# Turning the value matmuls of an attention kernel around (V stationary in four column groups, P streamed) and giving its scores 64 rows

## The chip, the cores and the metric

The kernel runs on one NeuronCore of a Trainium2 chip. The metric is the device time in microseconds, as the median of several executions. All times quoted here are of runs in the normal ("fast") state. Before the change the median was 1947.76 us (two runs, 1946.03 to 1949.48).

Abbreviations: PE is the TensorE (matmuls), PEld its weight loads, DVE the VectorE, ACT the ScalarE, POOL the GpSimd. PSUM is the memory that matmuls write; the kernel uses it as eight banks of 128 x 512 fp32.

## The reference, cut to what matters

```python
def _A_ref(x, wq, wk, wv, wo):           # S = 2048, D = 512, H = 32 heads, Dh = 16
    q = heads(x @ wq); k = x @ wk; v = x @ wv      # one k and one v for all 32 heads
    scores = einsum("bhqd,bkd->bhqk", q, k) * Dh ** -0.5
    p = softmax(scores)
    o = einsum("bhqk,bkd->bhqd", p, v)
    return merge(o) @ wo
# _B_ref: linear attention with H = 32 (cheap); _layernorm in front of each
x = x + A(ln(x));  x = x + B(ln(x));  x = x + A(ln(x));  x = x + B(ln(x))
```

Block A has 2048 x 2048 x 32 exponentials, twice. With 128 keys on the partitions and 512 queries in the free dimension that is 4096 tiles of 128 x 512: each is one score matmul, one exponential, and the value matmuls that consume it.

## The kernel before

A list scheduler in Python simulates the engines at build time with assumed durations, and so fixes the order of instructions on every engine. The order is static on the chip: if an engine is later than the scheduler assumed, the others wait (in `a_moreD` below the PE waits 65 us for the DVE to free score banks).

An exponential has two paths. ACT takes three score tiles at a time (`fill`). The DVE takes pairs of tiles with a polynomial in six passes (`dstep`, `dpass`); whoever is free in the scheduler's simulation takes the next tile.

```python
def smm(self, e, p, b):                       # one score tile: K of 32 rows
    u, kt, j = self.pos[p]
    qb, g, par = self.units[u]
    return e.matmul(bank(b), lhsT=Kr[32 * j:32 * j + 32, par, kt * P:(kt + 1) * P],
                    rhs=QT[32 * j:32 * j + 32, qb % 2, g, :], start=True, stop=True)
...
    def f(e):                                 # in fill: three scores, side by side in the array
        for i, p in enumerate(got):
            k = self.smm(e, p, 3 * s + i)
        return k
    o = add(PE, 0.06 + 0.08 * m, f, reads=self.keys(got), deps=prev, uses=[h], prio=0.0, name="sA")
    ...
    oe = add(AC, tac(m * 512), lambda e: e.activation(PTA[:, hp.idx, 0:m * 512], bank(3 * s, m * 512), ACTF.Exp, scale=SCALE), ...)
...
    def f(e):                                 # in add_pv: P is stationary, V (17 columns) moves
        first = opened[0]
        for qs in range(4):
            i = e.matmul(bank(7, 17, (qs * 4 + j) * 17), lhsT=src(qs), rhs=Vaug[:, kt, 0:17],
                         start=(first and qs == 0), stop=(qs == 3), skip_group_check=True)
        return i
...
    # in norm, after 64 tiles: reciprocal of column 17, product into Osb, from bank 7
```

A head has 16 rows of K. `Kr` holds K with zeros in the rows of the other head of a 32-row strip, so `par` chooses the head.

The softmax here doesn't subtract the row's maximum and nothing guards it: scores larger than these inputs give would overflow.

## Time and profile before

| | before |
|---|---|
| median | 1947.76 us |
| profiled span | 1935.7 us |
| mean granted TensorE clock | 0.575 |
| PE / DVE / ACT busy | 92% / 88% / 88% |
| exponentials on ACT; tiles on the DVE | 1179; 560 |
| idle time of ACT just before exponentials | 117.7 us |

Three views of the page of the kernel before follow. The first lines are busy time and share of each engine, and the granted clock in 40 slices of the span, in tenths of full speed.

```profile
span 1935.7 us, 49030 instructions
...
PE 1778.2 (92%) x22208; PEld 820.9 (42%) x22208; DVE 1712.9 (88%) x3063; ACT 1702.0 (88%) x1330; POOL 45.1 (2%) x77
...
PEclk8555556555665555555975555655565555556559
```

The chain that ended last, by engine:

```profile
PE 57%; DVE 29%; ACT 11%; issue 1%; DMA 0%; POOL 0%; SPq 0%
```

The groups of instructions (line, engine, operation, tiles, shapes, count | busy us, mean ns | idle us of the engine just before, and what ended it):

```profile
L689 ACT ACTIVATE PTA<-ps_all 128x1536 bf16<-128x1536 f32 x1179 | 1625.1, 1464 | 117.7 <-PE ps_all L572 108.8
L572 PE MATMUL ps_all<-QT,Kr 32*128 32x512 bf16 x4096 | 914.0, 582 | 80.0 <-ACT PTA L689 38.8
...
L608 PE MATMUL ps_all<-Vaug,PTA 128*128 128x17 bf16 x14144 | 584.0, 176 | 4.6 <-ACT PTA L689 2.5
L735 DVE TENSOR_SCALAR xT<-ps_all 128x512 int32<-128x512 f32 x560 | 385.1, 688 | 116.1 <-PE ps_all L572 105.1
...
L815 ACT ACTIVATE e_buf<-ps_all 128x512 f32<-128x512 f32 x64 | 37.8, 597 | 39.8 <-PE ps_all L475 38.7
```

Both users of the scores, ACT (L689) and the DVE (L735), idle over 100 us each for score matmuls, and the PE is first in the chain. Yet the TensorE clock is at half speed nearly all the time (digits 5 and 6, mean 0.575). So a slow PE delays two engines that would otherwise be nearly full.

The timeline of the PE at half clock shows what each piece takes (start us, us, engine, line, operation, count):

```profile
150.05 0.61 PE L572 MATMUL ps_all<-QT,Kr 32*128 32x512 bf16 x3
150.59 0.49 PE L608 MATMUL ps_all<-Vaug,PTA 128*128 128x17 bf16 x12
151.01 0.60 PE L572 MATMUL ps_all<-QT,Kr 32*128 32x512 bf16 x1
```

Three 32-row scores take 0.61 us and one takes 0.60: the three run side by side. Subtracting starts, a triple keeps the PE 0.54 us and its twelve value matmuls 0.42 us.

### The profile page before, as it was taken

To read this page: it belongs to the slowest core of one execution; us is meant where nothing else is said; L and a number is where in the kernel's file an instruction comes from. 1 tells how busy PE (TensorE), PEld (TensorE's weight loads), DVE (VectorE), ACT (ScalarE), POOL (GpSimd) and SP (SyncE) were. 2 spreads that over 40 slices of the span, in tenths; PEclk is the share of its full clock that TensorE was granted. 3 is DMA by queue.
4 is the path that set the end of the run, shared out by engine and by line. 5 is a ranking of instruction groups with operands and counts; after the bars stand their busy time and mean duration, and the time that the engine had idled before them with its cause. 6 is when DMAs were issued, how large, how long until landed. Compare 5 with 4: busy or idle time off the path is not lost.

```text
span 1935.7 us, 49030 instructions
## 1 busy us (share of the span) xinstructions
PE 1778.2 (92%) x22208; PEld 820.9 (42%) x22208; DVE 1712.9 (88%) x3063; ACT 1702.0 (88%) x1330; POOL 45.1 (2%) x77
## 2 busy tenths in 40 slices
PE   7999999999999999998889999999999999997977
PEld 4444444444444444443444444444444444443434
DVE  7899989999889988887879999899898989985977
ACT  6999999999989999997589999999998999986973
POOL 2000000000000000000100000000000000000000
PEclk8555556555665555555975555655565555556559
DMA  3000000000000000000000000000000000000001
GB/s 110 2 1 2 2 1 2 2 2 2 1 2 2 2 1 2 2 2 2 1 2 2 2 2 2 2 2 2 1 2 1 2 1 2 2 2 1 2 1 44
DMA packets 7808, 10.50 MB, mean 5 GB/s; under 512 B 1456, under 2 KB 7088, under 8 KB 7600
## 3 DMA queue, kind: packets, MB, share of 16 engines
q1 hardware_dynamic: 7600, 7.37, 1.2%
q8 instruction: 173, 2.83, 0.6%
q14 instruction: 35, 0.29, 0.0%
HBM read 5.28 MB, written 2.10 MB: 4 GB/s over the span
## 4 chain that ended last, share of the span: by engine, by line
PE 57%; DVE 29%; ACT 11%; issue 1%; DMA 0%; POOL 0%; SPq 0%
PE ps_all L572 27%; PE ps_all L608 16%; PE ps_all L475 11%; ACT PTA L689 10%; DVE xT L735 8%; DVE PTD L756 6%; DVE xu L751 3%; DVE xs L755 2%; DVE xs L752 2%; DVE xu L754 1%; DVE xs L753 1%; PE ps_all L920 1%; DVE stats L444 1%; PE ps_all L458 1%; DVE x_sb L931 1%
## 5 line engine op out<-in xcount | busy, mean ns | idle before, releaser
L689 ACT ACTIVATE PTA<-ps_all 128x1536 bf16<-128x1536 f32 x1179 | 1625.1, 1464 | 117.7 <-PE ps_all L572 108.8
L572 PE MATMUL ps_all<-QT,Kr 32*128 32x512 bf16 x4096 | 914.0, 582 | 80.0 <-ACT PTA L689 38.8
L608 PEld LDWEIGHTS ps_all<-Vaug,PTA 128*128 128x128 bf16 x14144 | 470.3, 104 | 566.0 <-issue 552.6
L608 PE MATMUL ps_all<-Vaug,PTA 128*128 128x17 bf16 x14144 | 584.0, 176 | 4.6 <-ACT PTA L689 2.5
L735 DVE TENSOR_SCALAR xT<-ps_all 128x512 int32<-128x512 f32 x560 | 385.1, 688 | 116.1 <-PE ps_all L572 105.1
L756 DVE SCALAR_TENSOR_TENSOR PTD<-xT,xs 128x1024 uint16<-128x1024 int32 x280 | 340.5, 1216 | 1.1
L572 PEld LDWEIGHTS ps_all<-QT,Kr 32*128 32x128 bf16 x4096 | 160.0, 98 | 311.6 <-ACT PTA L689 152.6
L751 DVE TENSOR_SCALAR xu<-xT 128x1024 f16<-128x1024 uint16 x280 | 192.3, 687 | 3.1
L755 DVE TENSOR_TENSOR xs<-xs,xu 128x1024 f16<-128x1024 f16 x280 | 191.0, 682 | 1.4
L752 DVE TENSOR_TENSOR xs<-xu 128x1024 f16<-128x1024 f16 x280 | 190.4, 680 | 0.5
L608 PE MATMUL ps_all<-Vaug,PTD 128*128 128x17 bf16 x2240 | 111.6, 176 | 16.6 <-DVE Osb L625 8.0
L753 DVE TENSOR_SCALAR xs<-xs 128x1024 f16<-128x1024 f16 x280 | 116.4, 416 | 1.0
L754 DVE TENSOR_SCALAR xu<-xu 128x1024 f16<-128x1024 f16 x280 | 117.0, 418 | 0.0
L608 PEld LDWEIGHTS ps_all<-Vaug,PTD 128*128 128x128 bf16 x2240 | 86.1, 104 | 66.8 <-DVE Osb L625 26.9
L475 PE MATMUL ps_all<-wqkv_sb,xnT 128*128 128x512 bf16 x256 | 106.3, 559 | 2.6 <-ACT xnT L464 1.4
L448 POOL TENSOR_TENSOR rstd<-veps,mhalf 128x1 f32<-128x1 f32 x64 | 40.9, 643 | 1842.2 <-DVE veps L446 1623.6
L815 ACT ACTIVATE e_buf<-ps_all 128x512 f32<-128x512 f32 x64 | 37.8, 597 | 39.8 <-PE ps_all L475 38.7
L475 PE MATMUL ps_all<-xnT,wq_sb 128*128 128x512 bf16 x128 | 55.8, 566 | 4.4 <-DVE xT L735 2.1
L475 PE MATMUL ps_all<-xnT,wqkv_sb 128*128 128x512 bf16 x128 | 52.4, 545 | 6.5 <-DVE pqT L818 5.6
L475 PE MATMUL ps_all<-wo_sb,OT 128*128 128x512 bf16 x128 | 51.9, 543 | 2.9 <-ACT OT L799 1.4
L444 DVE BATCH_NORM_STATS2 stats<-x_sb 128x6 f32<-128x512 bf16 x64 | 43.2, 683 | 3.5 <-DMA x_sb<-in_A_x_dram 3.3
L458 PE MATMUL ps_all<-ident,xn_buf 128*128 128x128 bf16 x256 | 31.2, 267 | 15.3 <-DVE xn_buf L451 13.6
(64 smaller groups left out, 625.9 us busy)
## 6 DMA issues: line engine op xcount, KB each, us to landing
out_dram<-x_sb SPq DMA_DIRECT2D x16, 128.0 KB, 1.7
x_sb<-in_A_x_dram SPq DMA_DIRECT2D x3, 512.0 KB, 7.3
wqkv_sb<-in_B_wqkv_dram SPq DMA_DIRECT2D x1, 1536.0 KB, 11.3
x_sb<-in_A_x_dram SPq DMA_DIRECT2D x2, 256.0 KB, 3.5
wq_sb<-in_A_wq_dram SPq DMA_DIRECT2D x1, 512.0 KB, 5.5
wo_sb<-in_A_wo_dram SPq DMA_DIRECT2D x1, 512.0 KB, 8.5
wo_sb<-in_B_wo_dram SPq DMA_DIRECT2D x1, 512.0 KB, 10.9
wk_sb<-in_A_wk_dram SPq DMA_DIRECT2D x1, 16.0 KB, 2.7
```

The source lines that it names most:

```text
L444: add(DV, tdv(512), lambda e: e.bn_stats(stats[:, t, 0:6], x_sb[:, t, :]), reads=[("x", t)], writes=[("st", t)], prio=prio, name="bn")
L475: i = e.matmul(bank(h.idx, n), lhsT=l, rhs=r, start=(c + k == 0), stop=(c + k == len(mms) - 1))
L572: return e.matmul(bank(b), lhsT=Kr[32 * j:32 * j + 32, par, kt * P:(kt + 1) * P], rhs=QT[32 * j:32 * j + 32, qb % 2, g, :], start=True, st ...
L608: i = e.matmul(bank(7, 17, (qs * 4 + j) * 17), lhsT=src(qs), rhs=Vaug[:, kt, 0:17], start=(first and qs == 0), stop=(qs == 3), skip_group_ ...
L689: oe = add(AC, tac(m * 512), lambda e: e.activation(PTA[:, hp.idx, 0:m * 512], bank(3 * s, m * 512), ACTF.Exp, scale=SCALE), deps=[o] + pr ...
L735: o = add(DV, tdv(512), lambda e: e.tensor_scalar(out=xT[:, hx.idx, i * 512:(i + 1) * 512], in0=bank(6), scalar1=SCALE * LOG2E * 65536.0, ...
L751: o = add(DV, tdv(1024, 0.52), lambda e: e.tensor_scalar(out=u_, in0=lo, scalar1=1.0 / 65536, scalar2=-0.5, op0=ALU.mult, op1=ALU.add), de ...
L752: o1 = add(DV, tdv(1024, 0.52), lambda e: e.tensor_tensor(out=s_, in0=u_, in1=u_, op=ALU.mult), deps=[o] + c["prev"], name="xsq", **kw)
L753: o2 = add(DV, tdv(1024, 0.26), lambda e: e.tensor_scalar(out=s_, in0=s_, scalar1=XK, scalar2=-XW, op0=ALU.mult, op1=ALU.add), deps=[o1], ...
L754: o3 = add(DV, tdv(1024, 0.26), lambda e: e.tensor_scalar(out=u_, in0=u_, scalar1=1.0, scalar2=XL, op0=ALU.mult, op1=ALU.add), deps=[o1], ...
L755: o4 = add(DV, tdv(1024, 0.52), lambda e: e.tensor_tensor(out=s_, in0=s_, in1=u_, op=ALU.mult), deps=[o2, o3], name="xc", **kw)
L756: o5 = add(DV, tdv(1024), lambda e: e.scalar_tensor_tensor(out=PTD[:, hp.idx, :].bitcast(U16), in0=xT[:, k, :], scalar=2.0 ** -9, in1=s_, ...
```

## The change

The value matmuls swap operands. V (16 columns, a column of ones and zeros up to 32) becomes the stationary operand in one of four groups of 32 columns of the array, and P streams 512 columns past it. That turns four matmuls per tile into one and is meant to let tiles of different column groups overlap (in the changed kernel three of them take 0.40 us). The result is O transposed, so after 64 tiles the bank is copied to SBUF in fp32, transposed by the PE in fp32, and only then normalised. The scores get 64 rows: K has 64-row strips with zeros in the rows of the other three heads, so only two score matmuls fit side by side instead of three or four. Some buffers shrink to make room.

```diff
-            return e.matmul(bank(b), lhsT=Kr[32 * j:32 * j + 32, par, kt * P:(kt + 1) * P],
-                            rhs=QT[32 * j:32 * j + 32, qb % 2, g, :], start=True, stop=True)
+            i, m = (j % NRG, par * (4 // NRG) + j // NRG)          # RG = 64, NRG = 2
+            r = slice(i * RG, (i + 1) * RG)
+            return e.matmul(bank(b), lhsT=Kr[r, m, kt * P:(kt + 1) * P], rhs=QT[r, qb % 2, g, :], start=True, stop=True)
...
-                for qs in range(4):
-                    i = e.matmul(bank(7, 17, (qs * 4 + j) * 17), lhsT=src(qs), rhs=Vaug[:, kt, 0:17],
-                                 start=(first and qs == 0), stop=(qs == 3), skip_group_check=True)
-                return i
-            o = add(PE, 0.15, f, ...)
+                c = (j % NRG) * (4 // NRG) + j // NRG
+                return e.matmul(ps[32 * c:32 * c + 32, 7 * 512:8 * 512], lhsT=Vaug[:, kt, :], rhs=src, start=opened[0], stop=opened[1],
+                                skip_group_check=True)
+            o = add(PE, 0.1, f, ...)
...  # norm: reciprocal and product came straight from bank 7; now first
+            oe = add((DV, AC), {DV: tdv(512), AC: tac(512)}, ev, deps=[last], acq=[he], uses=[h7], rel=[h7], prio=0.0, name="evA")
+            def tr(e):
+                for qs in range(4):
+                    i = e.transpose(bank(ht.idx, P, qs * P), Eo[:, he.idx, qs * P:(qs + 1) * P], identf[:])
+                return i
...
-            o = add(PE, 0.06 + 0.08 * m, f, ..., name="sA")
+            o = add(PE, 0.05 + 0.14 * m, f, ..., name="sA")
...  # also: four masked copies of K instead of two, smaller buffers, small rules for the
...  # spare PSUM bank and for odd tiles on the DVE, a switch for dummy matmuls (DUMMY = 0.0: off)
```

## The prediction

> **What bounds it now.** In the main attention stretch (100 to 890 us, table by stretches) PE is busy 94%, ACT 93%, DVE 92%, and the granted TensorE clock is 0.54. The groups show 1179 exponentials on ACT, 1625 us busy (1.378 us apiece), with 118 us idle before them, 109 of it waiting for the score matmuls; the DVE's score evictions wait another 105 us for scores. So ACT and DVE carry the exponentials and a slow-clocked PE delays both. The chain of waits gives PE 57%.
>
> [...] The trace agrees: only 0.5 and 1.0 occur, in multiples of 3.41 us. Counting matmuls per window, and weighting a 512-column matmul by the share of array rows that it uses (a score 0.25, a 17-column value matmul 0.033), windows under 5 full matmuls are practically never followed by a full clock (3 of 407), those over 6 usually are. Attention windows hold 3 to 4: hence the half clock.
>
> **What changes.**
> - Value matmuls: 16384 (twelve take 0.42 us at half clock) become 4096 of 512 columns, in four column groups. [...] the trace shows it for rows (three 32-row scores 0.61 us, one 0.60). So three should take one stream: 0.43 us at half clock, 0.22 at full.
> - Scores: only two fit side by side now, so a triple goes from one stream to two: 0.54 to about 0.97 us at half clock, 0.55 at full.
> - [...] I expect the full clock most of the time: mean 0.85 (0.7 to 0.98).
> - PE work per exponential, with projections (estimate): about 2.1 us at half clock, against 1.5 us observed per exponential today; about 1.25 us at full clock. The change stands or falls with the clock.
> - Instruction order: ACT gets 1202 exponentials (+23, +31 us) and 19 more key evictions (+9); DVE loses 63 score tiles (5.48 us per pair, -172 us) and gains 62 fp32 evacuations (0.69 us, +43) and 13 key evictions (+6). ACT's busy time goes to about 1740 us, DVE's to about 1590.
> - 256 fp32 transposes (estimate: [...] off the critical path at full clock).
>
> **Sum.** ACT 1740 + about 116 us of idle outside the exponentials (ends of layers, unchanged) + remaining waits before exponentials, falling from 118 to about 40, gives a span near 1896 us; the timed runs lie about 10 us above the profiled span. Even with no wait at all it would be 1856, so the gain cannot much exceed 4%.
>
> Predicted 1905 us, range 1866 to 1990; faster by over 2%: 0.46, within 2%: 0.33, slower: 0.21.
>
> **What shows it right or wrong.** Mean clock above 0.8 in the attention stretches; score triples near 0.55 us start to value matmul; value triples overlapping fully; idle before exponentials under 60 us, with PE busy about 80%; ACT share 91 to 93%; PE leaving first place in the chain of waits.
>
> **What would make it wrong.** Column groups counting little as activity, so that the clock keeps falling back: [...] at clock 0.6 the time passes 2100. Column groups not overlapping. The accumulator bank now waits for the fp32 copy and the transposes take the spare bank from the DVE path, stalling value matmuls between units. Or the waits before exponentials are not the PE's speed but its fixed order, and stay: then about 1950.

The clock of 0.85 stands as my estimate. The sum at the end: 1740 + 116 + 40 = 1896 us, and about 10 us more for the timed runs. The stream times can be read from the trace of before: four scores in two streams take 1.03 us where three side by side take 0.61, so a stream adds 0.42 us at half clock; at full clock it is 0.60 against 0.39, so 0.21. The estimates of the PE's work per exponential add the projections to the pieces above them. A recount of the windows of that trace has 1 of 400 under 5 followed by a full clock and 69 of 90 over 6; the half-clock windows of the attention stretches hold 4.0 on average.

## The result, and the profile after

The changed kernel takes 1849.78 us (two runs, 1845.92 and 1853.63): 0.9497 of the time before, with a 95% interval of 0.9405 to 0.9589. A later measurement of the same kernel with five runs gave 0.9528 (0.9505 to 0.9551). The direction was right; the time lies 16 us under the stated range, 55 us under the point.

The same lines of the page, for the changed kernel:

```profile
span 1844.2 us, 24784 instructions
...
PE 1608.2 (87%) x10093; PEld 463.8 (25%) x10176; DVE 1617.8 (88%) x2890; ACT 1714.6 (93%) x1373; POOL 47.7 (3%) x80
...
PEclk9999999999999999989999999999999999999999
```

The chain that ended last, by engine:

```profile
DVE 44%; ACT 31%; PE 22%; issue 2%; DMA 0%; POOL 0%; SPq 0%
```

The groups:

```profile
L722 ACT ACTIVATE PTA<-ps_all 128x1536 bf16<-128x1536 f32 x1202 | 1641.8, 1511 | 41.0 <-PE ps_all L590 37.8
L590 PE MATMUL ps_all<-QT,Kr 64*128 64x512 bf16 x4096 | 850.6, 387 | 126.7 <-ACT PTA L722 64.6
L625 PE MATMUL ps_all<-PTA,Vaug 128*32 128x512 bf16 x3599 | 524.9, 392 | 7.0 <-DVE Eo L637 4.5
L776 DVE TENSOR_SCALAR xT<-ps_all 128x512 int32<-128x512 f32 x497 | 341.7, 687 | 83.7 <-PE ps_all L590 82.2
...
L871 ACT ACTIVATE e_buf<-ps_all 128x512 f32<-128x512 f32 x64 | 43.3, 680 | 14.8 <-PE ps_all L490 10.6
...
L646 PE MATMUL ps_all<-identf,Eo 128*128 128x128 f32 x256 | 46.6, 310 | 7.0 <-DVE Eo L637 5.0
```

The clock is now full in almost every slice (mean 0.983 against 0.575). ACT does 23 exponentials more than before and still the time falls, because its idle time before them fell from 117.7 to 41.0 us. The PE left first place in the chain.

The timeline of the PE:

```profile
601.86 0.40 PE L625 MATMUL ps_all<-PTA,Vaug 128*32 128x512 bf16 x3
602.19 0.60 PE L590 MATMUL ps_all<-QT,Kr 64*128 64x512 bf16 x3
602.72 0.40 PE L625 MATMUL ps_all<-PTA,Vaug 128*32 128x512 bf16 x3
```

A triple of 64-row scores keeps the PE 0.53 us, as long as the triple of 32-row scores did at half clock, though it is two streams now. Three value matmuls finish in 0.40 us from first start to last end, about what one score takes alone at full clock (0.39 us in the run a_rg32 below): the column groups overlap. From its first start to that of the next score, a value triple keeps the PE 0.33 us (601.86 to 602.19).

**Where the time came from.** Cutting the span at the first and last exponential of each layer, the two attention stretches went from 889.7 + 917.2 = 1806.9 us to 851.3 + 862.5 = 1713.8 us, 93 us less. The rest of the span (start, between the layers, end) went from 128.8 to 130.4 us. So all of the gain lies inside the attention stretches. There ACT's busy time rose by 11 us and its idle time fell from 146.5 to 42.3 us.

### The profile page after: what moved, and what is told of

Its sections match the earlier page's. It is cut to its first block, busy times and chain, and to the rows that moved or that the text cites. A ratio compares the mean times of both kernels' runs of the same rounds, so it can differ in the third digit from the quotient of the medians.

```text
span 1844.2 us, 24784 instructions
## 1 busy us (share of the span) xinstructions
PE 1608.2 (87%) x10093; PEld 463.8 (25%) x10176; DVE 1617.8 (88%) x2890; ACT 1714.6 (93%) x1373; POOL 47.7 (3%) x80
## 4 chain that ended last, share of the span: by engine, by line
DVE 44%; ACT 31%; PE 22%; issue 2%; DMA 0%; POOL 0%; SPq 0%
ACT PTA L722 29%; DVE xT L776 10%; PE ps_all L590 9%; DVE PTD L798 8%; PE ps_all L625 6%; DVE xs L794 5%; DVE xs L797 5%; DVE xu L793 5%; PE ps_all L490 4%; DVE xu L796 3%; DVE xs L795 2%; PE ps_all L976 1%; PE ps_all L646 1%; DVE Eo L637 1%; ACT e_buf L871 1%
## 5 line engine op out<-in xcount | busy, mean ns | idle before, releaser
L590 PE MATMUL ps_all<-QT,Kr 64*128 64x512 bf16 x4096 | 850.6, 387 | 126.7 <-ACT PTA L722 64.6
L625 PE MATMUL ps_all<-PTA,Vaug 128*32 128x512 bf16 x3599 | 524.9, 392 | 7.0 <-DVE Eo L637 4.5
L590 PEld LDWEIGHTS ps_all<-QT,Kr 64*128 64x128 bf16 x4096 | 176.5, 94 | 574.2 <-ACT PTA L722 251.0
L798 DVE SCALAR_TENSOR_TENSOR PTD<-xT,xs 128x1024 uint16<-128x1024 int32 (+1 forms) x249 | 302.7, 1216 | 1.8
L625 PEld LDWEIGHTS ps_all<-PTA,Vaug 128*32 128x32 bf16 x3599 | 126.0, 93 | 483.2 <-issue 463.9
L793 DVE TENSOR_SCALAR xu<-xT 128x1024 f16<-128x1024 uint16 (+1 forms) x249 | 171.7, 689 | 4.2
L797 DVE TENSOR_TENSOR xs<-xs,xu 128x1024 f16<-128x1024 f16 (+1 forms) x249 | 170.7, 685 | 2.9
L794 DVE TENSOR_TENSOR xs<-xu 128x1024 f16<-128x1024 f16 (+1 forms) x249 | 170.4, 684 | 3.1
L625 PE MATMUL ps_all<-PTD,Vaug 128*32 128x512 bf16 x497 | 136.6, 396 | 31.9 <-DVE PTD L798 18.4
L796 DVE TENSOR_SCALAR xu<-xu 128x1024 f16<-128x1024 f16 (+1 forms) x249 | 104.4, 419 | 0.0
L871 ACT ACTIVATE e_buf<-ps_all 128x512 f32<-128x512 f32 x64 | 43.3, 680 | 14.8 <-PE ps_all L490 10.6
L646 PE MATMUL ps_all<-identf,Eo 128*128 128x128 f32 x256 | 46.6, 310 | 7.0 <-DVE Eo L637 5.0
```

The source lines that it names most:

```text
L590: return e.matmul(bank(b), lhsT=Kr[r, m, kt * P:(kt + 1) * P], rhs=QT[r, qb % 2, g, :], start=True, stop=True)
L625: return e.matmul(ps[32 * c:32 * c + 32, 7 * 512:8 * 512], lhsT=Vaug[:, kt, :], rhs=src, start=opened[0], stop=opened[1], skip_group_check ...
L646: i = e.transpose(bank(ht.idx, P, qs * P), Eo[:, he.idx, qs * P:(qs + 1) * P], identf[:])
L793: o = add(DV, tdv(w, 0.52), lambda e: e.tensor_scalar(out=u_, in0=lo, scalar1=1.0 / 65536, scalar2=-0.5, op0=ALU.mult, op1=ALU.add), deps= ...
L794: o1 = add(DV, tdv(w, 0.52), lambda e: e.tensor_tensor(out=s_, in0=u_, in1=u_, op=ALU.mult), deps=[o] + c["prev"], name="xsq", **kw)
L796: o3 = add(DV, tdv(w, 0.26), lambda e: e.tensor_scalar(out=u_, in0=u_, scalar1=1.0, scalar2=XL, op0=ALU.mult, op1=ALU.add), deps=[o1], nam ...
```

## The experiments

Twelve runs were made, in three jobs: eleven other kernels, and the changed kernel once more (`a_ctl`). The kernel before was timed in each job and had a median of 1939 to 1940 us there. The quoted expectations were put on record before each run. Most set two explanations against each other: the "clock theory" (the gain comes from the full TensorE clock, and the clock follows from how much of the array is at work) and a "rival".

### Each half of the change alone: a_rg32 and b_rg64

`a_rg32` is the changed kernel with 32-row scores again.

```diff
-    RG = 64
+    RG = 32
```

> The changed kernel with its scores back at 32 rows (three scores side by side again, one stream per triple instead of two); value matmuls and instruction order stay (1201 exponentials, 498 DVE score tiles against 1202 and 497). Clock theory (the gain came from the full clock, which the doubled row use of the scores holds): [...] the mean clock falls to 0.5 to 0.65 and the time rises to 1900 to 2050 us, although the PE has fewer streams to do. Rival (fewer and better shaped value matmuls made the gain, whatever the clock): the PE has less work than in the changed kernel, so 1835 to 1860 us.

Measured: 1957.01 us, 1.009 of before (1.0054 to 1.0127), clock 0.766, correct. The turned-around value matmuls alone bring nothing. The clock fell less than expected, but the time is where the clock theory put it, and the rival is off by 100 us. The order of instructions did not stay quite the same: with two masked copies of K instead of four, ACT has 11 instructions fewer and the DVE 21. But a_rg32 has the split of tiles and the scheduler rules of the changed kernel, so these alone do not make its gain. The page shows a clock that comes and goes, and ACT's wait for scores back:

```profile
PEclk8756589867887668958987666998569785787759
```

```profile
L722 ACT ACTIVATE PTA<-ps_all 128x1536 bf16<-128x1536 f32 x1201 | 1656.9, 1489 | 126.7 <-PE ps_all L590 118.6
```

`b_rg64` is the kernel before with 64-row scores alone: `smm`, the masked copies of K and the dependency keys as in the changed kernel. To make room, the buffers PTA, e_buf, xn_buf and Osb2/OT2 are one smaller each.

```diff
+    RG = 64
+    NRG, NM = P // RG, RG // DH
...
+            i, m = (j % NRG, par * (4 // NRG) + j // NRG)
+            r = slice(i * RG, (i + 1) * RG)
+            return e.matmul(bank(b), lhsT=Kr[r, m, kt * P:(kt + 1) * P], rhs=QT[r, qb % 2, g, :], start=True, stop=True)
```

> The kernel before with 64-row scores alone (four masked keys instead of two, value matmuls as before; some buffers one smaller to make room: PTA 5, e_buf 2, xn_buf 2, Osb2/OT2 2; 1182 exponentials, 558 DVE tiles). Clock theory: [...] the clock is unsteady between 0.6 and 0.95 and the time 1850 to 1990 us. Rival (value matmuls made the gain): 64-row scores only add a stream per triple, so slower than before, over 1990 us.

Measured: 2105.66 us, 1.0847 of before (1.0805 to 1.0889), clock 0.686. The output is wrong (relative error 0.21): I had left the order of the heads in the output as it was, while the 64-row strips permute the heads. The work is the same, so only the time is used. It is slower than I gave it credit for: here the prediction of the clock theory (1850 to 1990 us) was wrong and the rival's "over 1990" right. At half clock an exponential took 1.872 us, against 1.533 in before (table below), and the clock stayed at half for two thirds of the attention time (665 exponentials at 1.872 us, 462 at 1.360):

```profile
PEclk8655567565777668755797555679778775767659
```

So of the two halves one costs 1% and the other 8%, and both together gain 5%. The next runs test whether the clock is what joins them.

### Adding useless work: a_rg32_dum, b_dum160

`a_rg32_dum` adds to a_rg32 a matmul with zeros behind every value matmul (the diff leaves out two matmuls at the start, which clear the bank's columns and repeat the first value matmul).

```diff
                 e.matmul(ps[32 * c:32 * c + 32, 7 * 512:8 * 512], lhsT=Vaug[:, kt, :], rhs=src, ...)
+                return e.matmul(bank(7, 160, 272), lhsT=ident[:], rhs=zer[:, 0:160], start=False, stop=True, ...)
```

> The same with one useless 128-row matmul of 160 columns of zeros behind each value matmul (4096 more PE instructions[...]). Clock theory: the clock comes back to over 0.9 and the time to 1840 to 1875 us. If zeros do not count as activity, the clock stays under 0.65 and the time goes above the run without them, 1950 to 2150 us. Rival (PE work decides): slower than the 32-row run without it by 50 us or more.

Measured: 2869.98 us, 1.4793 of before, clock 0.997. This experiment was badly made. The clock was indeed full, but the filler stands between the value matmuls and takes away their overlap, as its timeline shows:

```profile
500.82 0.39 PE L628 MATMUL ps_all<-PTD,Vaug 128*32 128x512 bf16 x1
501.14 0.24 PE L635 MATMUL ps_all<-zer,ident 128*128 128x160 bf16 x1
501.31 0.39 PE L628 MATMUL ps_all<-PTA,Vaug 128*32 128x512 bf16 x1
```

A value matmul now occupies the PE for 0.32 us until the filler starts, and the filler for 0.17 us, so three pairs take 1.47 us. In the kernel before, a further 512-column stream adds 0.21 us at full clock (four scores of which the fourth has no free rows take 0.60 us where three take 0.39, below). Here 0.32 us pass; the trace does not show what the other 0.11 us go to.

```profile
494.28 0.39 PE L572 MATMUL ps_all<-QT,Kr 32*128 32x512 bf16 x3
495.68 0.60 PE L572 MATMUL ps_all<-QT,Kr 32*128 32x512 bf16 x4 [0.61 <-DVE x_sb L809]
```

The run shows that a full clock alone did not help a PE with too much to do: an exponential took 2.27 us at full clock, against 1.366 in a_rg32. It also bears on the question of the zeros: the clock was 0.997 with the filler of zeros and 0.766 without it (a_rg32). So the zeros did not keep the clock at half; that they are what raised it was not shown, since the PE's order of work changed with them.

`b_dum160` adds a filler with real data to the kernel before, where the value matmuls use the whole array anyway. The order of instructions is that of before on every engine.

```diff
-                return i
+                return e.matmul(bank(7, 160, 272), lhsT=ident[:], rhs=wq_sb[:, 0, 0:160], start=False, stop=True, ...)
```

> The kernel before, same order on every engine, with one useless 128-row matmul of 160 columns (weights as data, written to unused columns of the accumulator bank) behind each of the 4096 groups of value matmuls. Clock theory: [...] clock over 0.9, and the kernel gets faster by adding work: 1830 to 1880 us. Rival (the turned-around value matmuls made the gain): the PE was 92% busy, so added work costs time: 1970 to 2150 us.

Measured: 2090.41 us, 1.0764 of before (1.0718 to 1.0809), clock 0.73, correct.

```profile
PEclk9755556977879668876977555978558886895559
```

The clock rose (0.73 against 0.575) but did not stay, and the filler cost PE time: at half clock a group of four value matmuls with its filler kept the PE 0.24 us (0.17 at full), where without it twelve take 0.42, so four 0.14. As a test of the clock alone on the kernel before it failed; the rival's number came out.

### The same work twice: a_rg32_tw, with b_tw as its control

A filler that costs the PE about what the 64-row scores cost is to compute each 32-row triple twice into the same banks: two streams (0.61 us at full clock in this run, as against 0.60 for a 64-row triple in the changed kernel), and as many rows of the array in use, with no useful result in the second.

```diff
-                for i, p in enumerate(got):
-                    k = self.smm(e, p, 3 * s + i)
+                for _ in range(2):
+                    for i, p in enumerate(got):
+                        k = self.smm(e, p, 3 * s + i)
```

> The changed kernel with 32-row scores as in the run a_rg32 (1957 us, clock 0.77), but each ACT score triple is computed twice into the same banks: two streams per triple as in the changed kernel, and the same activity, by pure repetition (about 3600 useless score matmuls). Clock theory: the activity of the changed kernel is back, so the clock is over 0.93 and the time 1840 to 1880 us, faster than a_rg32 by doing the same work twice. Rival (PE work decides, or the 64-row tiles themselves matter): the second pass costs the PE 0.22 to 0.43 us per triple, so 2000 us or more.

Measured: 1874.08 us, 0.9646 of before (0.9599 to 0.9693), clock 0.963, correct. The kernel became 83 us faster than a_rg32 by doing 3598 score matmuls a second time. The rival expected 2000 us or more. Its page, against that of a_rg32 above:

```profile
PEclk9999999999999999998989998999889999899989
```

```profile
L723 ACT ACTIVATE PTA<-ps_all 128x1536 bf16<-128x1536 f32 x1201 | 1645.2, 1502 | 62.0 <-PE ps_all L590 56.9
L590 PE MATMUL ps_all<-QT,Kr 32*128 32x512 bf16 x7694 | 880.0, 389 | 114.2 <-ACT PTA L723 56.6
```

The order of the ACT's and the DVE's instructions is that of a_rg32 from first to last, and the results are right; what differs is the repetition, the clock, and ACT's wait, which halves from 126.7 to 62.0 us. (The two ran in different jobs; their ratios to before, 0.9646 and 1.009, say the same.) It stays 24 us slower than the changed kernel, at a clock of 0.963 against 0.98; why was not tested.

`b_tw` does the same to the kernel before, with its own buffers and right outputs.

> The kernel before, same order on every engine, ACT score triples computed twice: what 64 rows would do to streams and activity, with right outputs and the buffers of before. Control for b_rg64 (2106 us, clock 0.69, smaller buffers, heads of the output permuted). If buffers had no part in it: 2060 to 2140 us, clock 0.6 to 0.75. If the smaller buffers were the cause of its loss: under 1990 us.

Measured: 2181.49 us, 1.1259 of before (1.1211 to 1.1308), clock 0.617, correct. It is slower than the range I gave, but it answers its question: with buffers of full size the second stream costs even more, so the loss of b_rg64 needs no smaller buffers to explain it. With the old value matmuls, more work in the scores did not lift the clock for good (0.617 here, 0.686 in b_rg64, 0.575 in before):

```profile
PEclk8555565556566667755985555755567675555559
```

### The clock within a run

One kernel has both clocks in one execution, with the same order of instructions. Inside the attention stretches (30 us after the first exponential of a layer to 20 us before its last), the trace's records of the clock and of the exponentials give this time per exponential of ACT:

```
               at half clock: us per exponential (count)     at full clock
before         1.533 (1023)                                  1.412 (96)
b_rg64         1.872 (665)                                   1.360 (462)
b_tw           1.862 (865)                                   1.358 (259)
b_dum160       1.912 (550)                                   1.401 (573)
a_rg32         1.688 (505)                                   1.366 (638)
a_rg32_tw      2.35  (48)                                    1.395 (1091)
changed        2.57  (18)                                    1.393 (1124)
```

At the full clock these seven run at nearly the same pace, 1.36 to 1.41 us, though their matmuls differ in shape. At the half clock they differ a lot, from 1.533 to 2.57 us. The half-clock figures of the changed kernel and of a_rg32_tw must not be read as a cost of the clock alone: they rest on 18 and 48 exponentials, and cause and effect run both ways, since the clock also falls where the PE has stalled (in the changed kernel the PE was busy 61% of the window before each of the eight falls in these stretches, 89% of the other full-clock windows). Nor is a full clock enough by itself: at full clock a_rg32_dum takes 2.27 us per exponential, and a_moreD below 1.48. So the change does not make the PE's work cheaper; it makes the PE's clock nearly full (0.983), and at that clock the PE kept up with ACT whether its work was a little more or less (1.366 us per exponential in a_rg32, 1.393 in the changed kernel).

### What the clock went with

The records of the clock hold 0.5 and 1.0 alone, in pieces of 3.41 us or multiples (traces of before and after). How busy the PE is does not set the two apart: in the attention stretches it is busy 94% of the half-clock windows of before, and 89% of the full-clock windows of the changed kernel. In the trace of before the clock went with the work in a window. I counted the matmuls that start in each, in units of 512 columns, weighted by the share of the array's rows that they use, as in the prediction. Of the windows under 5, 1 of 400 was followed by a full clock; from 5 to 6 it was 9 of 72, over 6 it was 69 of 90.

The runs that differ in their matmuls have these mean clocks:

| | old value matmuls | turned around |
|---|---|---|
| 32-row scores | 0.575 (before) | 0.766 (a_rg32) |
| 64-row scores | 0.686 (b_rg64) | 0.983 (changed) |
| 32-row scores, ACT's triples twice | 0.617 (b_tw) | 0.963 (a_rg32_tw) |

So either half of the change raised the clock, but it was nearly full only where the value matmuls were turned around and the scores had 64 rows or were done twice. How much a matmul of each shape counts, and in particular how the 32 columns of a value matmul do, was not shown. That the clock follows the share of the array at work, and not, say, power, is my inference.

### What bounds the kernel now: a_fewD and a_moreD

`a_fewD` tells the scheduler that DVE operations take 1.3 times as long. The chip's DVE is the same; only the split and the order change.

```diff
-        return 0.065 + n * c * 1e-3
+        return 1.3 * (0.065 + n * c * 1e-3)
```

> The changed kernel with the scheduler told that DVE operations take 1.3 times as long, so that its order gives the DVE 396 score tiles instead of 497, and ACT about 1233 exponentials instead of 1202. Theory (at the full clock ACT alone bounds the attention stretch, at 1.33 to 1.37 us per exponential): 31.5 times that, so 40 to 45 us more, 1880 to 1900 us. Rival (PE or DVE still bound it): within 15 us of the changed kernel, or faster since the DVE has 276 us less to do.

Measured: 1888.96 us, 0.9748 of before (0.9723 to 0.9772), clock 0.966, correct. Its span is 45 us longer than that of the changed kernel, for 33 exponentials more (the profile counts 1235), though the DVE's busy time fell by 234 us to 1383.5 us. Of these 45 us, 31 lie in the attention stretches and 14 outside, where the altered durations change the order too. That the total fell into the range is thus partly luck: in the attention stretches 33 exponentials cost 0.94 us each, less than the 1.33 to 1.37 of the theory, because ACT's idle time there fell too, from 42.3 to 35.9 us. The rival is refuted all the same: with 234 us less for the DVE to do the kernel became slower, and the chain that ended last is now ACT's:

```profile
ACT 83%; PE 14%; DVE 2%; issue 1%; DMA 0%; SPq 0%; POOL 0%
```

In the changed kernel the chain names the DVE first (44%), yet ACT is busy in 97.5% of the attention stretches (1671.5 of 1713.8 us), so ACT bounds them.

`a_moreD` uses a factor of 0.9 instead: 536 tiles on the DVE.

> The changed kernel with the scheduler told that DVE operations take 0.9 of its estimate: 536 score tiles on the DVE instead of 497 and 1189 exponentials on ACT instead of 1202. Theory (ACT bounds at 1.33 to 1.37 us per exponential): 13 fewer, so 15 to 18 us faster, if the DVE keeps up; its busy time goes from 1618 to about 1725 us. Rival (DVE is nearly full too, 90% busy in the attention stretch): the gain is lost to waits, 0 to 10 us slower.

Measured: 1970.99 us, 1.0169 of before (1.0128 to 1.0209), clock 0.957, correct. That is 120 us slower than the unaltered changed kernel, far beyond either theory. Its chain and its groups show where:

```profile
DVE 63%; PE 27%; ACT 6%; issue 3%; DMA 0%; POOL 0%; SPq 0%
```

```profile
L722 ACT ACTIVATE PTA<-ps_all 128x1536 bf16<-128x1536 f32 (+1 forms) x1189 | 1644.0, 1458 | 145.4 <-PE ps_all L590 137.2
L590 PE MATMUL ps_all<-QT,Kr 64*128 64x512 bf16 x4096 | 884.4, 395 | 140.2 <-DVE xT L776 65.0
...
L625 PE MATMUL ps_all<-PTD,Vaug 128*32 128x512 bf16 x536 | 145.5, 407 | 73.6 <-DVE PTD L798 46.9
```

ACT is idle 145 us before exponentials, 137 of them for scores, and the PE in turn waits for the DVE: 65 us for a score bank and 47 us for the DVE's probabilities (32.8 and 18.4 us in the changed kernel). The clock is nearly full. The PE takes its instructions in the fixed order, so where that order assumes a DVE that is quicker than the real one, a late DVE stops the PE and with it ACT: this is how I read the waits, not a test. How much of the loss is the DVE's load and how much the too hopeful order was not separated. Of the three splits tried, that of the changed kernel is the best, and moving 101 tiles off the DVE cost about 40 us where moving 39 tiles onto it (with an order that assumes a faster DVE) cost 120.

### The transposes: a_tr2, a_ctl, a_tbf16, a_comb

`a_tr2` does every fp32 transpose twice.

```diff
-                for qs in range(4):
-                    i = e.transpose(bank(ht.idx, P, qs * P), Eo[:, he.idx, qs * P:(qs + 1) * P], identf[:])
+                for qs in range(8):
+                    i = e.transpose(bank(ht.idx, P, qs % 4 * P), Eo[:, he.idx, qs % 4 * P:(qs % 4 + 1) * P], identf[:])
```

> The changed kernel with every fp32 transpose done twice into the same place (256 more, about 47 us of PE time by the trace). Theory: off the critical path at the full clock, so less than 0.7% (1837 to 1863 us). Rival: the transposes hold the spare bank that the DVE's scores need and stand in front of the value matmuls, so most of it is paid: 1875 us or more.

Measured: 1868.86 us, 0.9642 of before (0.9612 to 0.9672), correct. `a_ctl` is the changed kernel, unaltered, in the next job:

> The changed kernel itself, unaltered, timed beside the next three: 1838 to 1856 us, ratio to before 0.945 to 0.957.

Measured: 1850.54 us, 0.9528 (0.9505 to 0.9551), clock 0.98. The two were not in one job, but each has its own runs of before, and the intervals lie apart: the second set of transposes costs 18 us by the medians and 1.1% of before, some 22 us, by the ratios. By the profile the transposes' group keeps the PE busy for 80.5 us instead of 46.6, so 34 us more. So they are neither hidden, as I had predicted, nor paid in full.

`a_tbf16` holds the evacuated O^T and its transposes in bf16; the order of instructions is that of a_ctl.

```diff
-    Eo = sb("Eo", [P, 2, 512], FP32)
+    Eo = sb("Eo", [P, 2, 512], BF16)
...
-                    i = e.transpose(bank(ht.idx, P, qs * P), Eo[:, he.idx, qs * P:(qs + 1) * P], identf[:])
+                    i = e.transpose(bank_bf(ht.idx)[:, qs, :], Eo[:, he.idx, qs * P:(qs + 1) * P], ident[:])
```

> The changed kernel with the evacuated O^T and its transposes in bf16 instead of fp32, same order on every engine. Doubling the fp32 transposes had cost about 20 us, so they are not off the critical path as predicted; the trace gives them 47 us of PE busy time. Theory (the wait from the last value matmul to the freed banks is what costs): bf16 transposes are shorter, so 5 to 15 us faster than the unaltered one. Rival (the fp32 form is hidden): within 4 us.

Measured: 1840.28 us, 0.9493 of before (0.9472 to 0.9513), correct. The gain over a_ctl is 10 us in the medians and 0.35% of before in the ratios; the two intervals touch, so it is likely but not certain. It is the fastest kernel, and it rounds O to bf16 once more on the way. `a_comb` joins this to a_moreD:

> Both together. If both theories hold, 20 to 33 us faster than the unaltered changed kernel, about 1820 us; if only one holds, 5 to 18 us faster.

Measured: 1967.22 us, 1.0149 of before (1.0123 to 1.0175), correct: a_moreD's loss, whatever the transposes.

## Why the prediction was right or wrong, point by point

**Right: the clock.** "The change stands or falls with the clock" held. The traces have 0.5 and 1.0 alone, in pieces of 3.41 us. The prediction counted the matmuls in such windows by the share of rows that they use, read in the trace of before that windows with little are practically never followed by a full clock (3 of 407 in its count), and so had the right direction. The mean clock was 0.983 against the "0.85 (0.7 to 0.98)" of the prediction, just past the upper end; the step from the count to 0.85 was my estimate. In the experiments the same reckoning gave the size of the clock less well: for a_rg32 0.5 to 0.65 (measured 0.766), for b_dum160 over 0.9 (0.73), and for b_rg64 a time under 1990 us (2106).

**Right but for two: the pieces.** Score triples at 0.53 us (predicted 0.55), value triples overlapping, 1202 exponentials and 497 tiles, DVE busy 1617.8 us (predicted 1590), idle before exponentials 41.0 us (predicted 40), and the PE no longer first in the chain. The 40 is partly luck: the prediction shows no working for it and made it for a lower clock. Missed were the value triple's hold on the PE, 0.33 us and not 0.22, and with it the PE's busy share, 87% and not about 80%.

**Wrong: the sum.** The step that failed is this one, as the prediction put it: "ACT 1740 + about 116 us of idle outside the exponentials (ends of layers, unchanged) + remaining waits before exponentials, falling from 118 to about 40, gives a span near 1896 us", and with it "Even with no wait at all it would be 1856". The span was 1844.2 us, below that floor. By the profile the terms are 1714.6 + 88.6 + 41.0. The last was right; the first two were too large by 25 and 27 us, which is the whole error of 52 us. (The other 3 us of the 55 are the distance of the timed runs from the profiled span, 5.6 us and not 9.)

- *ACT's busy time.* I charged each exponential 1.378 us, the busy time over the count in the kernel before (1625.1 / 1179). That mean mixes exponentials that follow one another with ones that start after a wait. In both traces consecutive exponentials of full size start as little as 1.330 us apart, while one instruction's typical duration in before is 1.451 us: the start of one overlaps the end of the one before. The fewer waits, the more of them overlap. In before, 283 exponentials started after idle time of ACT and added 1.451 us each to its busy time, the other 896 added 1.352 on average; after, only 133 started after idle time, and the other 1069 added 1.345. So removing waits also lowers the busy time: all exponentials together added 8 us more (1621.6 to 1629.3), where I had charged 31 for the 23 new ones. The traces show the overlap, 1.451 less 1.330, about 0.12 us; I should have looked for it.
- *The idle time outside.* I called all 116 us that were not before an exponential "ends of layers, unchanged". The ends of the layers did stay: ACT's idle time there was 87.2 us before and 87.3 after. The other 29 us stood inside the attention stretches, in front of ACT's other instructions that wait for the PE: the group of L815 (now L871) had 39.8 us, 27.4 of it inside the stretches, and has 14.8, none of it inside. They were waits of the same kind as those before exponentials and went the same way. A look at the idle time by stretch instead of by subtraction would have shown it.

**Wrong in part: the transposes.** "Off the critical path at full clock" is not so: doubling them cost 18 to 22 us. (An estimate of their PE time is cut from the prediction, since it names no number that it comes from; they took 46.6 us.)

**Not tested on its own.** No kernel of mine raised the clock of the kernel before without burdening its PE; b_dum160 tried and failed. That the clock alone would have sped up that kernel rests on its 96 exponentials at full clock (1.412 against 1.533 us), and not on a run. For the changed kernel the cause is shown by a_rg32 and a_rg32_tw.

## What to carry to other kernels

Look at the granted clock before you count the PE's work: here a PE that was 92% busy had a mean clock of 0.575, and once the value matmuls were turned around, padding the scores with zero rows was worth more than saving streams (1850 us at clock 0.983 against 1957 at 0.766). Two parts of a change can each lose and yet win together, as here, where the clock was 0.766 and 0.686 with one of them and 0.983 with both; so test the parts and the whole. When waits go away, take the price of an instruction from its back-to-back distance, not from its mean in a trace full of waits, and read idle time by stretch before calling a part of it fixed.
